# Changing the order of two TensorE products at the ends of triples in a fused attention and SwiGLU kernel

## The chip, the cores and the metric

The kernel runs on one core of one Trainium2 chip. The metric is the device time of one execution in microseconds (us), the median over several runs. A profile comes from one further execution, recorded by the hardware profiler; its span runs from the first to the last instruction. TensorE does the matrix products into PSUM banks, ScalarE (ACT in the profile) and VectorE (DVE) move and combine results, GpSimd (POOL) does small fills, and SyncE (SP) issues most DMAs.

## The reference

Two blocks follow each other. The first is a gated linear attention: per batch and head a 48 x 48 state decays by a sigmoid gate, takes in an outer product of k and v, and is read by q. The second is a SwiGLU feed-forward block on the attention's output, 3072 tokens of 384 features, with 1536 hidden features. All is float32.

```
def _attn_ref(q, k, v, f_logit):          # (4, 8, 768, 48) each
    f = 1.0 / (1.0 + np.exp(-f_logit))
    for t in range(S):
        state = f[:, :, t, :, None] * state + einsum('bhd,bhe->bhde', k[:, :, t], v[:, :, t])
        y[:, :, t] = einsum('bhd,bhde->bhe', q[:, :, t], state)

def _moe_ref(x, w_gate, w_val, w_out):    # x: (3072, 384), from y
    g = x @ w_gate
    silu = g * (1.0 / (1.0 + np.exp(-g)))
    return (silu * (x @ w_val)) @ w_out
```

## The kernel before

The sequence of 768 steps is cut into six chunks of 128 steps. A chunk of all four batches has 512 tokens. Attention works on one unit (one batch and one chunk) at a time, as a Python generator (`attention`, line 528) that hands out its work in small steps. The feed-forward block of a chunk follows one chunk or so behind, so that its matrix products fill TensorE while ScalarE and VectorE work on the attention of later chunks. Chunk 0 goes through `mlp_plain` in the usual way; chunks 1 to 5 go through `mlp_fifteen` (line 908), and it is there that the change is made.

`mlp_fifteen` computes the gate and value products with a fast scheme for a 3 x 3 by 3 x 2 block product: instead of 18 block products it makes 15, from sums of weight blocks and sums of token blocks made beforehand, and then combines the 15 results by additions into six blocks. One set of 15 is called a triple here (function `triple`, line 941); each chunk has `NJ` = 4 triples, numbered j and taken in the order 0, 2, 1, 3. The 15 products are r = 0 to 14, listed in `PRODUCTS` (line 897): each names a bank (A, B, o or c), a weight sum and a token sum. One product is four matmul records in the trace (two halves, each float32 matmul in two passes), all from line 954.

A product either opens a bank (the first use of its name in the triple, and every "o") or adds onto what is already in it. So bank A of a triple collects r0, r3, r6, r9, r12 and r14 in turn, and in between ScalarE copies its running sum out: to `c11` after r0, to `c12` after r3, and to a scratch tile `aside` after r6, r9 and r12 (line 959). Bank B is used in the same way by r1, r4, r7, r10 and r13. The next product on a bank has to wait until the copy of the one before has read it. The end of a triple and the start of the next are:

```
r12  A  a32 x t11   then ScalarE: copy A to aside
r13  B  e1 x t3     then ScalarE: copy B to aside
r14  A  a22 x b21   the bank itself is the result, read in the next triple
r0   A  a11 x t14   of the next triple, in the other A bank; then ScalarE: copy A to c11
r1   B  a23 x t8    of the next triple; then ScalarE: copy B to c22
```

There are two A banks, one B bank, two banks for o and c together, and three further banks for the attention. A bank of A is free again when the silu (line 970) and the product with it (line 906) of its triple's last result have read it; these are put off into the next triple (`late`, popped after the products in `FINISH`). Additions on VectorE that follow a product are put off by one piece (`lag`, line 905).

The order of work is written out by hand. `pieces` (line 1024) is the list of the products of a chunk's four triples; the seven products of the down projection (`down_seven`, lines 1053 and 1116) follow. Each piece has a nominal duration (`PRODUCT` = 0.86). A loop at the end of `short_path` (lines 1271 to 1280) walks through the pieces with a clock `now` that adds these up, and before each piece it lets in the attention steps whose due time has come (`come_in`). The due times are in `SCORES`, `CHAINS` and `times` (lines 825 to 841). Seven of the ends of triples inside a chunk are such due times (`between`): there the output products y (lines 649 and 653), the state products dS (694), the score products sc (615) and in the earlier chunks the transposes kt (619) come in, together with a sigmoid on ScalarE (555) that has to load its function table first, the copies of y (657), and on VectorE the mask on the scores (628) and a transpose of the sigmoid's output (561). `in_order` then fixes, for each of TensorE, VectorE, ScalarE, GpSimd and SyncE, exactly the order in which the instructions were written.

```
    now = 0.0
    for c in range(1, NCH):
        come_in(now)
        for took, f in blocks[c]:
            come_in(now)
            before = lagging[:]
            lagging.clear()
            f()
            for g in before:
                g()
            now += took
```

Of the kernel before, what the change touches and what calls it, by code (L numbers as in the profile page):

```python
# [289 lines left out]
def short_path(ctx, tc, ident, least, judge, q, k, v, f_logit, moe_w_gate, moe_w_val, moe_w_out, out):  # L290
# [595 lines left out]
    def down_weight_sums():  # L886
# [4 lines left out]
        for i in (1, 2, 4):  # L891
# [5 lines left out]
    PRODUCTS = [("A", "a11", "t14"), ("B", "a23", "t8"), ("o", "a21", "b22"),  # L897
                ("A", "a12", "t2"), ("B", "e3", "b32"), ("o", "e0", "t1"),
                ("A", "e5", "t9"), ("B", "e2", "t5"), ("c", "a13", "b11"),
                ("A", "e4", "t4"), ("B", "a33", "t15"), ("c", "a31", "t10"),  # L900
                ("A", "a32", "t11"), ("B", "e1", "t3"), ("A", "a22", "b21")]
# [3 lines left out]
    def lag(f, *args):  # L905
        lagging.append(lambda: f(*args))  # L906

    def mlp_fifteen(c):
# [28 lines left out]
        def out_part(i, n, j):  # L937
            f = i * NJ + j
            return hidden_tile(h, f % NP)[:, 2 * (f // NP) + n, :]

        def triple(j):
            p, got = {}, {}

            def both(name):
                return {"A": banks_a, "B": banks_b, "o": banks_o, "c": banks_o}[name].tile(
                    [128, 512], FP32, tag=name if name in "AB" else "o", name=name).rearrange("p (n t) -> p n t", n=2)

            def product(r):
                name, a, b = PRODUCTS[r]
                fresh = name == "o" or name not in p  # L950
                if fresh:
                    p[name] = both(name)
                for n in range(2):
                    nc.tensor.matmul(p[name][:, n, :], lhsT=weights_of[a][:, n, j, :], rhs=tokens[b],  # L954
                                     start=fresh and n == 0, stop=True, skip_group_check=True)

            def copy(name, tag, **kw):
                t = comb.tile([128, 2, TH], FP32, tag=tag, name=tag, **kw)
                nc.scalar.copy(t, p[name])  # L959
                return t  # L960

            def aside(name):
                return copy(name, "aside", bufs=3)

            def finish(i, n, src):


                def f():
                    dst = out_part(i, n, j)
                    nc.scalar.activation(dst, src[:, 0, :], AF.Silu)  # L970
                    lag(nc.vector.tensor_tensor, dst, dst, src[:, 1, :], ALU.mult)
                late.append(f)

            def one_product(r):
                product(r)
                if r in FINISH and late:
                    late.pop(0)()
                if r == 0:
                    got[11] = copy("A", "c11", bufs=2)
                elif r == 1:  # L980
                    got[22] = copy("B", "c22")
                elif r == 2:
                    lag(minus, got[22], p["o"], got[22])
                elif r == 3:
                    got[12] = copy("A", "c12")
                elif r == 4:
                    lag(plus, got[12], got[12], aside("B"))
                elif r == 5:
                    lag(minus, got[12], p["o"], got[12])
                elif r == 6:  # L990
                    lag(minus, got[22], got[22], aside("A"))
                elif r == 7:
                    got[32] = copy("B", "c32")
                elif r == 8:
                    got[31] = copy("c", "c31")
                    finish(0, 1, got[12])
                    finish(1, 1, got[22])
                elif r == 9:
                    lag(plus, got[32], got[32], aside("A"))
                elif r == 10:  # L1000
                    lag(minus, got[31], got[31], aside("B"))
                elif r == 11:
                    lag(minus, got[32], got[32], p["c"])
                    finish(2, 1, got[32])
                elif r == 12:
                    lag(minus, got[31], got[31], aside("A"))
                    finish(2, 0, got[31])
                elif r == 13:
                    lag(plus, got[11], got[11], aside("B"))
                    finish(0, 0, got[11])  # L1010
                else:
                    finish(1, 0, p["A"])

            return [(PRODUCT, lambda n=n: one_product(n)) for n in range(len(PRODUCTS))]
# [7 lines left out]
        hidden_sums, last = down_seven(c, h)  # L1022
        order = list(range(0, NJ, 2)) + list(range(1, NJ, 2))
        pieces = [f for j in order for f in triple(j)]
        half = len(PRODUCTS) * (NJ // 2)
        pieces.insert(half + 12, (0, lambda: lag(hidden_sums, 0)))
        pieces += [(0, finish_late), last[0], (0, lambda: lag(hidden_sums, 1))]
# [234 lines left out]
    def tokens_of(c):  # L1262
        token_sums, blocks[c] = mlp_fifteen(c)
        token_sums()
# [95 lines left out]
```

## Time and profile before

| | |
|---|---|
| median of 6 runs | 613.82 us (613.76 to 615.03) |
| the profiled execution | 615.0 us |
| its span | 613.3 us |
| TensorE's granted clock, mean | 0.996 |
| products of line 954 | 300, in 20 triples of 15, from 148.1 to 580.2 us |
| ScalarE's copies of line 959 | 0.58 us each |
| moved by DMA | 54.10 MB |

The page gives for each engine the time in which it ran an instruction, as a share of the span. PEld is the loading of weights, which can run while an earlier matmul is still going. The chain of waits is followed back from the last instruction: it names, at each moment, the engine that held up the end. Lines of the order of time have the start, the duration, the engine, the line, the operation, what is written and read, its shape, how many instructions are merged, and in brackets how long the engine was idle before it and what ended this.

The triples take these parts of the span, by the starts of their products: chunk 1 from 148.1 to 208.3, chunk 2 from 247.3 to 308.9, chunk 3 from 343.2 to 402.8, chunk 4 from 437.0 to 495.7 and chunk 5 from 527.8 to 580.2 us. In chunk 5 no attention is left.

### The profile page before, as it was taken

The numbers are of one execution on the slowest core, as the hardware profiler recorded it, in microseconds if no ns is written. First come the engines' busy times: TensorE is split into PE (matmuls) and PEld (weight loads), VectorE is DVE, ScalarE is ACT, GpSimd is POOL, SyncE is SP. The second block draws the span as 40 slices with busy tenths as digits, with TensorE's granted clock in tenths as the row PEclk, the third lists the DMA queues.
The fourth block names the chain that finished last, engine by engine and source line by source line (L and its number), as shares of the span: only waits on it lengthen the run. The fifth ranks groups of instructions, "written<-read, shape, count | busy, mean of one in ns | idle before, by whom it ended". The sixth has DMA issues, their size and how long they took to land.

```text
span 613.3 us, 10812 instructions
## 1 busy us (share of the span) xinstructions
PE 597.2 (97%) x4036; PEld 489.5 (80%) x4036; DVE 499.5 (81%) x882; ACT 285.3 (47%) x526; POOL 7.6 (1%) x51
## 2 busy tenths in 40 slices
PE   7799999999999999999999999999999999999996
PEld 5654545666888799888899988899988889988896
DVE  7799989878999996989997889996879992566731
ACT  2375646312776520576731376641276730366600
POOL 1000000000000000000000000000000000000000
PEclk9899999999999999999999999999999999999999
DMA  9999582005322134324235344144313100100001
GB/s 148 247 210 285 174 249 79 1 14 154 85 55 69 27 92 120 114 53 96 52 96 129 100 102 115 30 115 117 109 44 93 27 5 10 52 2 2 0 1 58
DMA packets 109142, 54.10 MB, mean 88 GB/s; under 512 B 68760, under 2 KB 102168, under 8 KB 109080
## 3 DMA queue, kind: packets, MB, share of 16 engines
q1 hardware_dynamic: 107064, 50.56, 34.7%
q10 hardware_dynamic: 2016, 2.75, 1.3%
q8 instruction: 34, 0.56, 0.4%
q14 instruction: 28, 0.23, 0.1%
HBM read 44.04 MB, written 6.29 MB: 82 GB/s over the span
## 4 chain that ended last, share of the span: by engine, by line
PE 84%; DVE 7%; DMA 3%; ACT 2%; issue 1%; SPq 1%; ACTq 0%; DVEq 0%
PE o L1053 19%; PE A L954 14%; PE B L954 11%; PE gate L752 5%; PE val L752 5%; PE o L775 5%; PE o L954 5%; PE c L954 4%; PE sc L615 4%; PE o L1116 3%; PE y L653 2%; PE y L674 2%; PE dS L694 1%; PE y L649 1%; DVE c L858 1%
## 5 line engine op out<-in xcount | busy, mean ns | idle before, releaser
L954 PE MATMUL A<-xs,w_both 128*128 128x256 f32 x240 | 62.5, 383 | 1.1 <-ACT aside L959 1.1
L1053 PE MATMUL o<-w_out,h 128*128 128x192 f32 x360 | 62.0, 328 | 0.5 <-DVE h L906 0.5
L1053 PEld LDWEIGHTS o<-w_out,h 128*128 128x128 f32 x360 | 58.7, 190 | 1.7 <-DVE h L906 0.8
L959 ACT COPY c<-A 128x512 f32<-128x512 f32 x40 | 23.3, 583 | 66.2 <-PE A L954 66.2
L954 PEld LDWEIGHTS A<-xs,w_both 128*128 128x128 f32 x240 | 44.6, 190 | 9.0 <-ACT aside L959 2.8
L855 DVE TENSOR_TENSOR c<-c,aside 128x512 f32<-128x512 f32 x60 | 41.6, 693 | 9.8 <-ACT aside L959 8.4
L959 ACT COPY aside<-A 128x512 f32<-128x512 f32 x60 | 35.0, 583 | 28.9 <-PE A L954 28.9
L906 DVE TENSOR_TENSOR h<-h,c 128x256 f32<-128x256 f32 x100 | 41.2, 420 | 7.9 <-ACT h L970 7.7
L970 ACT ACTIVATE h<-c 128x256 f32<-128x256 f32 x100 | 39.2, 416 | 9.0 <-DVE c L855 5.8
L858 DVE TENSOR_TENSOR c<-c,aside 128x512 f32<-128x512 f32 x60 | 41.3, 689 | 2.0 <-ACT aside L959 1.7
L954 PE MATMUL B<-xs,w_both 128*128 128x256 f32 x160 | 41.2, 380 | 0.7 <-ACT aside L959 0.7
L1053 PE MATMUL o<-ws,h 128*128 128x192 f32 x240 | 41.5, 328 | 0.2 <-DVE A L628 0.2
L954 PE MATMUL c<-xT,w_both 128*128 128x256 f32 x160 | 41.2, 380 | 0.5 <-DVE c L858 0.5
L954 PE MATMUL A<-xs,extra 128*128 128x256 f32 x160 | 41.2, 380 | 0.0
L954 PE MATMUL B<-xT,extra 128*128 128x256 f32 x160 | 41.1, 380 | 0.0
L959 ACT COPY aside<-B 128x512 f32<-128x512 f32 x60 | 35.0, 584 | 11.0 <-PE B L954 7.0
L628 DVE TENSOR_TENSOR A<-sc,causal 128x512 f32<-128x512 f32 x48 | 30.8, 682 | 11.2 <-PE sc L615 11.0
L1053 PEld LDWEIGHTS o<-ws,h 128*128 128x128 f32 x240 | 39.1, 190 | 0.8 <-DVE A L628 0.4
L858 DVE TENSOR_TENSOR c<-o,c 128x512 f32<-128x512 f32 x40 | 27.7, 693 | 10.2 <-ACT h L970 5.8
L954 PEld LDWEIGHTS B<-xs,w_both 128*128 128x128 f32 x160 | 30.3, 190 | 5.1 <-ACT aside L959 1.1
L954 PEld LDWEIGHTS c<-xT,w_both 128*128 128x128 f32 x160 | 30.3, 190 | 5.1 <-DVE c L858 0.9
L954 PEld LDWEIGHTS A<-xs,extra 128*128 128x128 f32 x160 | 30.3, 190 | 4.4 <-ACT c L959 0.3
(137 smaller groups left out, 1140.7 us busy)
## 6 DMA issues: line engine op xcount, KB each, us to landing
fsquares<-in_f_logit_dram SPq DMA_DIRECT2D x64, 96.0 KB, 2.7
ksquares<-in_k_dram SPq DMA_DIRECT2D x64, 96.0 KB, 2.5
qsquares<-in_q_dram SPq DMA_DIRECT2D x64, 96.0 KB, 2.2
v<-in_v_dram SPq DMA_DIRECT2D x24, 192.0 KB, 3.5
w<-in_moe_w_gate_dram SPq DMA_DIRECT2D x6, 768.0 KB, 6.1
w<-in_moe_w_val_dram SPq DMA_DIRECT2D x6, 768.0 KB, 5.4
w<-in_moe_w_out_dram SPq DMA_DIRECT2D x6, 768.0 KB, 5.6
out_dram<-ob ACTq DMA_DIRECT2D x14, 192.0 KB, 2.1
```

Source lines behind the costliest of these rows:

```text
L615: nc.tensor.matmul(sc[par][:, a * C:(a + 1) * C], lhsT=kT[r, a, :], rhs=qT[r, a, :], start=True, stop=True)
L628: nc.vector.tensor_tensor(A[:, par], sc[par].rearrange("p (a t) -> p a t", t=C), causal.unsqueeze(1).broadcast_to((128, HP, C)), ALU.mult)
L752: nc.tensor.matmul(p, lhsT=w[:, j, i, :], rhs=xT[c][:, i, :], start=(i == 0), stop=(i == KT - 1))
L775: nc.tensor.matmul(p, lhsT=hidden_tile(h, n // 2)[:, n % 2 * 2 + b // 2, b % 2 * C:(b % 2 + 1) * C], rhs=w_out[:, j, :], start=(n == 0), s ...
L855: nc.vector.tensor_tensor(dst, a, b, ALU.add)
L858: nc.vector.tensor_tensor(dst, a, b, ALU.subtract)
L906: lagging.append(lambda: f(*args))
L954: nc.tensor.matmul(p[name][:, n, :], lhsT=weights_of[a][:, n, j, :], rhs=tokens[b], start=fresh and n == 0, stop=True, skip_group_check=True)
L959: nc.scalar.copy(t, p[name])
L970: nc.scalar.activation(dst, src[:, 0, :], AF.Silu)
L1053: nc.tensor.matmul(p[:, n, :], lhsT=lhsTs[j][:, n * C:(n + 1) * C], rhs=rhs[:, j, :], start=first and j == order[0] and n == 0, stop=j == ...
L1116: nc.tensor.matmul(p, lhsT=hidden_tile(h, j)[:, 2, n * C:(n + 1) * C], rhs=b22[:, j, :], start=j == order[0], stop=j == order[-1])
```

## The change

At each end of a triple but the last of a chunk, the triple's last product r14 and the next triple's first product r0 change places in `pieces`. The new order is r12, r13, r0 of the next triple, r14, r1 of the next triple. Both have the same nominal duration, so the attention steps that came in between r14 and r0 now come in between r0 and r14. What a product brings with it moves too: the copy of r0's bank to `c11` is issued on ScalarE with r0, so ahead of the attention steps' ScalarE work; r14 issues nothing on another engine but appends a finish to `late`. There are 15 such ends. From line 1025 on, lines of the changed kernel have numbers higher by 3.

```
         pieces = [f for j in order for f in triple(j)]
+
+        for n in range(len(PRODUCTS), len(pieces), len(PRODUCTS)):
+            pieces[n - 1:n + 1] = pieces[n - 1:n + 1][::-1]
         half = len(PRODUCTS) * (NJ // 2)
         pieces.insert(half + 12, (0, lambda: lag(hidden_sums, 0)))
```

## The prediction

> **What bounds the kernel now.** I read the page's busy shares first, then the chain of waits, then what the weight loads wait for, then the order of time around the ends of triples.
>
> ```profile
> PE 597.2 (97%) x4036; PEld 489.5 (80%) x4036; DVE 499.5 (81%) x882; ACT 285.3 (47%) x526; POOL 7.6 (1%) x51
> ...
> PE 84%; DVE 7%; DMA 3%; ACT 2%; issue 1%; SPq 1%; ACTq 0%; DVEq 0%
> ```
>
> TensorE is busy for 97% of the span and carries 84% of the chain that ended last; VectorE is next. So a stall of TensorE in the triples counts in full, except where VectorE holds the pace. I number products r0 to r14 and triples 0 to 19, four for each of five token chunks. Triples 3, 7, 11, 15 and 19 are the last of their chunk and keep their order; 15 boundaries are swapped. The list of what the weight loads wait for has this row:
>
> ```profile
> PEld A L954 <- ACT aside L959: 7.7, 23, 0.7
> ```
>
> Its place is seen at the end of triple 17, where no attention work runs (order of time, all engines):
>
> ```profile
> 552.15 1.03 PE L954 MATMUL B<-xT,extra 128*128 128x256 f32 x4
> 552.40 0.58 ACT L959 COPY aside<-A 128x512 f32<-128x512 f32 x1 [1.20 <-PE A L954]
> ...
> 553.04 0.73 PEld L954 LDWEIGHTS A<-xT,w_both 128*128 128x128 f32 x4 [0.27 <-ACT aside L959]
> 553.04 1.13 PE L954 MATMUL A<-xT,w_both 128*128 128x256 f32 x4
> 553.21 0.58 ACT L959 COPY aside<-B 128x512 f32<-128x512 f32 x1 [0.22 <-PE B L954]
> ...
> 554.01 1.03 PE L954 MATMUL A<-xs,w_both 128*128 128x256 f32 x4
> ```
>
> r12 writes bank A and ScalarE copies it until 552.98; r14 adds to the same bank, with only r13 between. Its weights load at 553.04, when the copy is done, instead of about 0.21 ahead of its matmul as usual (551.93 before 552.15). From r13's start to the start after r14 are 1.86 us; two undisturbed products take 2 x 0.864 = 1.73 (the chain shows 0.86 for each r1 to r11). So this end costs 0.13 to 0.14: 0.03 of waiting and 0.10 because the next product starts with nothing loaded ahead. Where other work stands between r13 and r14 the cost is missing: the last product of triple 0 takes 0.87 (162.43 to 163.30) and of triple 16 0.88 (540.04 to 540.92). That ties it to the copy.
>
> **What the swap removes.** After r13 comes the next triple's r0, on the other A bank; then r14, with two products of cover. The copy ends 0.83 after r13 starts; r14 would now want to load at about 0.86 + 0.86 - 0.21 = 1.51 after it. Its wait goes.
>
> - Five boundaries without attention between (after triples 5, 9, 13, 17, 18): 0.14 each, 0.70.
> - Seven with attention between r14 and r0 (after triples 1, 4, 6, 8, 10, 12, 14): r13's start to the first y product is 1.96 (477.89 to 479.85). The r0 of triple 4 shows what an unstalled product before such a switch takes: 0.96 (247.25 to 248.21). So 0.864 + 0.96 = 1.82, gain 0.13 each, 0.91. The product after the attention pays the same entry after the scores (0.97) whether it is r0 or r14.
> - After triples 0 and 16: nothing to remove.
> - After triple 2: lost. There r1 of triple 3 starts at 195.21 whatever comes before, since its bank B is copied out only at 194.57 to 195.15, and that copy waited 2.14 for VectorE, which runs without a pause from 179.97. VectorE's start there waits for scores, so triple 1's gain passes through.
>
> Sum: 1.61 us.
>
> **What it adds on TensorE.** r0's new wait is for its A bank, freed by VectorE's product h<-h,A of the triple before. That ends 1.6 us (triple 1, 174.06 against 175.68) to 4.0 us (553.04 less 549.01) before r14's present start, where r0 will stand: cost 0, and a loss only if that cover shrank by 1.6. r1 still has r14 or r0 and r13's copy behind it, as now. No instruction is added; DMA issues keep their order, though SP's xT transfers wait on copies that come later (below), and xT is used only by a later chunk.
>
> **What it moves on ScalarE.** The c11 copy of r0 now enters ScalarE's queue before the sigmoid and the yT copies at the seven attention boundaries. Behind it wait a table load, the sigmoid, yT, and on VectorE the transpose that reads the sigmoid. Triple 14 is the tightest:
>
> ```profile
> 478.79 1.13 PE L954 MATMUL A<-xT,w_both 128*128 128x256 f32 x4
> 478.96 0.58 ACT L959 COPY aside<-B 128x512 f32<-128x512 f32 x1 [0.22 <-PE B L954]
> ...
> 479.56 1.28 ACT L555 ACT_TABLE_LOAD   x1
> ...
> 480.86 0.63 ACT L555 ACTIVATE fsquares<-fsquares 128x512 f32<-128x512 f32 x1
> 481.39 0.63 ACT L657 COPY yT<-y 128x256 f32<-128x256 f32 x2
> ...
> 481.58 1.11 DVE L561 STREAM_TRANSPOSE gates<-fsquares 128x512 f32<-128x512 f32 x1 [0.16 <-issue]
> ...
> 482.66 1.29 DVE L628 TENSOR_TENSOR A<-sc,causal 128x512 f32<-128x512 f32 x2
> ...
> 484.18 0.41 PEld L954 LDWEIGHTS o<-xT,w_both 128*128 128x128 f32 x2
> ```
>
> r0 will start at 477.89 + 0.86 = 478.75; its copy follows 1.07 later (as r13's: 477.89 to 478.96), at 479.82, and takes 0.60. The table load moves from 479.56 to 480.42, the sigmoid to 481.72, the transpose to 482.44, the first of the two masks to 483.52, ending (0.69 each, 0.60 apart) at 484.21. Its o bank is what r2 loads for, at 484.18 - 0.13 = 484.05. So r2 comes some 0.2 late in its load, which by the pattern of r14 costs about 0.12. I take 0.12, with 0 and 0.3 (the lateness plus a refill of 0.10) as ends. After triples 6 and 10 the same transpose stands before the mask, but TensorE does the dS products too (0.55, 264.19 to 264.74): the mask becomes free at about 390.77 against a load at 391.1: cost 0, end 0.2 each. After triples 1 and 4 the kt transposes reuse the y bank: yT's first half moves to about 265.41, kt wants it at 265.70: 0, end 0.1 each. After triples 8 and 12 the mask stands before the transpose. VectorE is then up to 0.5 late against TensorE in triples 7 and 11; the tightest reader is ScalarE's silu at 305.18, which delays the copy at 305.56 by some 0.3, and r13, which needs it, starts only at 307.08. In triple 15 VectorE has 0.68 idle before 485.88 to catch up.
>
> Net: 1.61 - 0.12 = 1.49, about 1.5 us. The profiled execution took 615.0 with a span of 613.3; by its own account it would become 613.5 with a span of 611.8. It is 1.2 slower than the median of 613.82, and taken off that median, 613.82 - 1.49 = 612.3.
>
> A rule of the Trainium skill speaks against the change. The page "ScalarE: Activation LUTs", section "What ACT_TABLE_LOAD costs", gives a switch of tables 1.28 us plus a drain of about 1.38, 2.66 in all. The row here has the load at 479.56 for 1.28 and the sigmoid at 480.86, with no drain between. With the page's sum in ScalarE's queue the mask would come 1.38 later after triples 6, 10 and 14, losing about 1.2, 1.2 and 1.7 with the refill, and kt some 1.2 twice: 6.5 lost against 1.6 gained, an estimate of 618.7. I go by the row.
>
> **The rivals.**
>
> 1. *The attention boundaries gain nothing (613.1).* If the later sigmoid and copies hold TensorE about as long as r14 did, only the plain 0.70 remains: 613.82 - 0.70. For it: the margins of 0.1 to 0.3 above, and VectorE at 81%. Against: only triple 14's margin is negative by these rows.
>
> 2. *Nothing changes (613.8).* If the 0.13 belonged to two successive products on A banks, or to r14's operands, the swap would keep it. Against: triples 0 and 16, where r14 goes at 0.87 to 0.88; for it: nothing but that those two have other work before them.
>
> 3. *Slower (615.1).* One mechanism: in-order ScalarE, at the ends of triples 6, 10 and 14. With c11 ahead of the sigmoid, transpose, mask and o bank are late and r2 waits. If the mask comes d later than worked out above, triples 7 and 11 lose d - 0.3 each, triple 15 loses d + 0.2, and each a refill of 0.10: 3d - 0.1 in all. That is more than the 1.61 gained from d = 0.57 on; at d = 1.0 it is 2.9, and the time 613.82 - 1.61 + 2.9 = 615.1. For it: the c11 copy could itself be late if r0 were held for its bank, and VectorE waits in order. Against: the bank is free 1.7 us ahead or more there, and every duration in the sum is from rows.
>
> **How the numbers follow.** Forecast 0.64, rival 1 0.20, rival 2 0.06, rival 3 0.10. The forecast's own range, from the ends (losses of 0 up to 0.3 + 0.4 + 0.2, or none and triple 2's 0.14 kept as well), is 612.1 to 613.1. The range of 611.6 to 613.6 takes in rival 1, and on the fast side half a us for what the lowest and the fifth of the six times of before differ by (613.76 and 614.25); it leaves out rival 3 and rival 2. About 0.2%, 1.2 us, is what a measurement tells from no change, so faster means below 612.6: the forecast gives 0.58 and rival 1 0.04, together 0.62; the same gets 0.29, slower 0.09.
>
> **What would show it.** In the profile after: aside-to-A waits of the weight loads fall from 23 to about 10 (13 swapped ends gone; the chunks' last triples keep theirs); r14's step is 0.86 or, after scores, 0.97; at 553 the two A products take 1.73 together; c11 copies stand before the sigmoids; a new wait of an o product for the mask in triple 15, about 0.2 long. Rows of r0 waiting for h<-h,A, of kt waiting for yT, or of o products waiting for masks in triples 7 and 11 would make the prediction wrong, as would steps of 0.97 that stay without a wait.

## The result, and the profile after

The changed kernel is faster by 0.22%: the ratio of its time to that of before is 0.9978, 95% interval 0.9973 to 0.9984 (36 and 74 runs, medians 613.63 and 614.79 us). In microseconds that is 1.0 to 1.7 less, 1.35 in the middle. The median of all 74 runs of the kernel before is higher than that of the first six, from which the prediction started (614.79 against 613.82), so the ratio is what counts: on the base of 613.82 it makes 612.5, where 612.3 was forecast. The plain ends alone, 0.70 us, would have made 0.9989, which lies outside the interval.

The page of the changed kernel, its busy times and its chain of waits:

```profile
span 611.1 us, 10812 instructions
...
PE 593.3 (97%) x4036; PEld 488.7 (80%) x4036; DVE 498.5 (82%) x882; ACT 285.6 (47%) x526; POOL 7.6 (1%) x51
...
PE 81%; DVE 10%; ACT 3%; DMA 2%; issue 2%; SPq 1%; ACTq 0%; DVEq 0%
```

TensorE still bounds the kernel; the count of instructions is the same. The list of what the weight loads wait for, of the kernel after:

```profile
PEld A L954 <- ACT aside L959: 4.1, 9, 0.7
```

Fourteen of the 23 waits of products on bank A for ScalarE's `aside` copies are gone, and 3.6 of 7.7 us. The end of triple 17 in the order of time, to be held against the same place before:

```profile
550.15 1.03 PE L954 MATMUL B<-xT,extra 128*128 128x256 f32 x4
550.40 0.58 ACT L959 COPY aside<-A 128x512 f32<-128x512 f32 x1 [1.20 <-PE A L954]
550.80 0.84 PEld L954 LDWEIGHTS A<-xs,w_both 128*128 128x128 f32 x4
551.01 1.03 PE L954 MATMUL A<-xs,w_both 128*128 128x256 f32 x4
...
551.66 0.84 PEld L954 LDWEIGHTS A<-xT,w_both 128*128 128x128 f32 x4
...
551.88 1.03 PE L954 MATMUL A<-xT,w_both 128*128 128x256 f32 x4
```

The copy of r12 ends at 550.98. r0 (A<-xs) runs meanwhile on the other A bank; r14 (A<-xT) loads at 551.66, 0.22 ahead of its matmul and with no wait in brackets. r13, r0 and r14 follow each other at 0.86 or 0.87.

How the stretch of the triples shrank, by the starts of products in the two traces (us; r13 of one triple to r1 of the next):

```
end of triple      1     2     4    5    6    8    9    10   12   13   14   16    17   18
shorter by         0.08  0.01  0.14 0.14 0.13 0.14 0.13 0.14 0.14 0.14 0.13 0.02  0.13 0.13
triple 0 to r13 of triple 19:   before 430.20    after 428.55    shorter by 1.65
```

The spans differ by 2.2, not 1.65: 0.62 of it lies ahead of the first triple, which began at 147.47 to 148.42 in the thirteen profiles of all these kernels, though no change is made before it; the stretch after r13 of triple 19, whose order is the same, was 0.13 longer, and 0.65 longer again in a second profile of the same changed kernel (35.07 and 35.72). So one span against another shows less than the ends one by one.

### The profile page after: what moved, and what is told of

Same layout as the page of the kernel before. It is cut to its first block, busy times and chain, and to the rows that moved or that the text cites. A ratio compares the mean times of both kernels' runs of the same rounds, so it can differ in the third digit from the quotient of the medians.

```text
span 611.1 us, 10812 instructions
## 1 busy us (share of the span) xinstructions
PE 593.3 (97%) x4036; PEld 488.7 (80%) x4036; DVE 498.5 (82%) x882; ACT 285.6 (47%) x526; POOL 7.6 (1%) x51
## 4 chain that ended last, share of the span: by engine, by line
PE 81%; DVE 10%; ACT 3%; DMA 2%; issue 2%; SPq 1%; ACTq 0%; DVEq 0%
PE o L1056 19%; PE A L954 14%; PE B L954 11%; PE o L954 5%; PE o L775 5%; PE val L752 4%; PE c L954 4%; PE sc L615 4%; PE gate L752 3%; PE o L1119 3%; PE y L653 2%; PE y L674 2%; PE y L649 1%; PE dS L694 1%; DVE c L858 1%
## 5 line engine op out<-in xcount | busy, mean ns | idle before, releaser
L959 ACT COPY c<-B 128x512 f32<-128x512 f32 x40 | 23.5, 586 | 26.3 <-PE B L954 22.9
```

## The experiments

They are read by the stretch from the first product of triple 0 to r13 of triple 19, and by the steps (start to start) of the products in it. Times are given as ratios to the kernel before on the same chip, with 95% intervals.

**The swap at a part of the ends.** First only where no attention comes in, then only where it does; `met` lists the latter by chunk, and the second kernel has `in met` in place of `not in met`.

```
+        met = {1: (2,), 2: (1, 3), 3: (1, 3), 4: (1, 3)}.get(c, ())
         for n in range(len(PRODUCTS), len(pieces), len(PRODUCTS)):
-            pieces[n - 1:n + 1] = pieces[n - 1:n + 1][::-1]
+            if n // len(PRODUCTS) not in met:
+                pieces[n - 1:n + 1] = pieces[n - 1:n + 1][::-1]
```

> The swap only at the eight ends of triples without attention between. I measure the stretch from the first product of triple 0 to r13 of triple 19: 430.21 us before, 428.55 with all ends swapped. Theory (r14's wait for ScalarE's copy of r12 goes, 0.14 where it was, nothing after triples 0, 2 and 16): -0.70, so 429.5, with each of the ends after triples 5, 9, 13, 17 and 18 shorter by 0.13 to 0.14. Rival (the gain comes from the c11 copy going ahead of the attention's work on ScalarE): 430.2. Time about 0.1% under before.

> The swap only at the seven ends with attention between. Theory: -0.95, so 429.25 for the same stretch, the ends after triples 4, 6, 8, 10, 12 and 14 shorter by 0.13 to 0.14 each and that after triple 1 by 0.08. Rival (the gain comes from ScalarE's order): all of the 1.66, 428.55. Time about 0.15% under before.

The first kernel took 429.36 (0.84 less), and its ratio is 0.9994 (0.9983 to 1.0005), which by itself is not clear of no change. The ends after triples 5, 9, 13, 17 and 18 ran r13, r0 and r14 at 0.86 each; the attention ends kept 0.89 to 0.92 from r13 to r14, and 1.03 to 1.06 from r14 to the first y product. The second took 429.05 (1.15 less), ratio 0.9983 (0.9972 to 0.9993), with the two groups exchanged. At the ends themselves the first gained 0.67 at those five and the second 0.81 at its seven, 0.06 instead of 0.14 at the one after triple 8; of the rest, 0.18 and 0.29 fell at the end of chunk 1, which varies from run to run (see below). So the two parts sit each in its own kind of end, and the ratios, 0.06% and 0.17%, together make about the whole. ScalarE's order is the same in the first kernel as before, instruction by instruction, so it can't have made the first group's gain.

**The suspected wait doubled, in both orders.** r12's bank is copied to `aside` a second time in all triples but the last of a chunk; the data are the same.

```
                 elif r == 12:
-                    lag(minus, got[31], got[31], aside("A"))
+                    t = aside("A")
+                    if j != 3:
+                        nc.scalar.copy(t, p["A"])
+                    lag(minus, got[31], got[31], t)
```

> Order of before; r12's copy is made twice in all triples but the last of a chunk. Theory (r14 waits for that copy): 0.58 more at each of the twelve ends that have the wait, 0.6 after triple 16, little after triples 0 and 2: 7.6 us, the stretch 437.8, the time 1.2% longer. Rival (0.13 is the price of two products on A banks in a row, or of r14's operands, and the copy does not hold it): within 0.3 of 430.2.

> Swapped order, r12's copy made twice in the same triples. Theory: with two products of cover the doubled copy ends 0.83 + 0.59 = 1.42 us after r13's start, before r14 loads at 1.52, so 428.6, at most 0.3 more through the attention ends, where r13's copy and c11 come 0.1 to 0.35 later. Rival (the swap only moves the wait): some 0.5 for each end, 434 or more.

In the old order the stretch grew by 8.0 to 438.23, ratio 1.0133 (1.0112 to 1.0153). The end of triple 17 in this kernel's order of time (L1008 is the second copy):

```profile
559.79 0.59 ACT L1008 COPY aside<-A 128x512 f32<-128x512 f32 x1
...
560.43 0.73 PEld L954 LDWEIGHTS A<-xT,w_both 128*128 128x128 f32 x4 [0.89 <-ACT aside L1008]
560.43 1.13 PE L954 MATMUL A<-xT,w_both 128*128 128x256 f32 x4 [0.48 <-ACT aside L1008]
...
561.40 1.03 PE L954 MATMUL A<-xs,w_both 128*128 128x256 f32 x4
```

r14 waits 0.89 instead of 0.27, and the step from r13 is 1.51 instead of 0.89. The difference of 0.62 is what one more copy takes, start to start (the first begins at 559.17, the second at 559.79). It came at all fourteen ends where r14 had waited; after triple 2 the next triple's r1 gave it back (the step into it fell from 1.76 to 1.15), so thirteen are left, which make 8.06. In the new order the same doubled copy, at the end of the same triple:

```profile
552.27 0.58 ACT L1008 COPY aside<-A 128x512 f32<-128x512 f32 x1
...
552.91 0.84 PEld L954 LDWEIGHTS A<-xT,w_both 128*128 128x128 f32 x4
553.12 1.03 PE L954 MATMUL A<-xT,w_both 128*128 128x256 f32 x4
```

The second copy ends at 552.85 and r14 loads at 552.91 without a wait: the two products of cover are just enough for two copies. All swapped ends kept the steps of the swapped kernel. The stretch was 429.53, 1.0 above the swapped kernel's 428.55 and so over my 0.3; against that kernel, product by product, 0.24 came in triple 1 (r11 behind the c copy), 0.24 at the end of chunk 1 (the diagonal wait, below) and 0.46 at a group of scores in chunk 2's down products (they wait for VectorE's qT), none at an end of a triple. Ratio 0.9986 (0.9974 to 0.9997).

**The c11 copy put back behind the attention's ScalarE work,** with TensorE's order as swapped.

```
+        held = []
...
+                while r == len(PRODUCTS) - 1 and held:
+                    held.pop(0)()
-                if r == 0:
+                if r == 0 and j:
+                    held.append(lambda: got.update({11: copy("A", "c11", bufs=2)}))
+                elif r == 0:
                     got[11] = copy("A", "c11", bufs=2)
```

> TensorE's order as swapped, but the c11 copy is issued on ScalarE with r14, so behind the attention's ScalarE work as before. Theory (TensorE's cover is the whole gain): the stretch of the triples stays at 428.55 within 0.1. Rival (ScalarE's order brings it): back to 430.2.

The stretch was 429.46, which is neither 428.55 nor 430.2. Product by product r13, r0 and r14 run at every end as in the swapped kernel; 0.71 of the 0.91 came at one place in chunk 1's down products and 0.21 at the scores after triple 8. The place, first in the swapped kernel and then in this one (weight loads in the order of time):

```profile
237.89 0.14 PEld L674 LDWEIGHTS y<-qT,diagonal 128*32 128x32 f32 x2 [0.24 <-ACT diagonal L545]
```

```profile
238.98 0.14 PEld L674 LDWEIGHTS y<-qT,diagonal 128*32 128x32 f32 x2 [0.95 <-ACT diagonal L545]
```

The `diagonal` tile shares its buffer with a yT tile, so its fill waits for the xT transfers that read yT; SyncE took 7.33 us to issue ten of them here and 6.46 there. The plain repeat of the swapped kernel had 0.56 at this place, so the same kernel varies here too. Its time is 0.9988 (0.9979 to 0.9997). By the ends the gain is TensorE's cover and not ScalarE's order; by the whole time alone this run would not have told.

**The c11 copy twice at the attention ends,** the mechanism of the slower rival.

```
                 if r == 0:
                     got[11] = copy("A", "c11", bufs=2)
+                    if j in {1: (1,), 2: (2, 3), 3: (2, 3), 4: (2, 3)}.get(c, ()):
+                        nc.scalar.copy(got[11], p["A"])
```

> Swapped order, the c11 copy made twice at the seven attention ends: sigmoid, yT, transpose and mask come 0.59 later. Theory of the slower rival in the prediction, with the margins that the changed kernel's trace shows: triple 15's r2 loads when the mask is done, so it loses about 0.6; in triples 7 and 11 the mask is 0.40 ahead, 0.2 to 0.3 lost each; kt after triples 1 and 4 has 0.26, about 0.3 and less lost; 1.6 in all, the stretch 430.1, the gain gone. If that queue does not reach TensorE: 428.55.

The stretch was 430.19 and the ratio 1.0010 (0.9999 to 1.0022): the gain is gone. The losses are where they were expected: 0.40 at kt after triple 1 and again after triple 4, 0.13 and 0.13 at r2 in triples 7 and 11, 0.59 at r2 in triple 15, 1.65 in all. The scores after triple 8 and those in chunk 2's down products lost 0.3 more, and the end of chunk 1 was 0.4 shorter. In triple 15 (order of time):

```profile
483.31 1.28 DVE L628 TENSOR_TENSOR A<-sc,causal 128x512 f32<-128x512 f32 x2
...
484.05 0.73 PEld L954 LDWEIGHTS o<-xT,w_both 128*128 128x128 f32 x4 [0.73 <-DVE A L628]
```

r2's load waits 0.73 for the mask. Of the delay of 0.59, 0.49 came into the step before r2, and the other 0.10 is the step after it, which begins with nothing loaded ahead. So the path over ScalarE's queue, the sigmoid and VectorE's transpose reaches TensorE, and the swapped kernel stands only some 0.1 us from it in triple 15.

**The last triples too.** A chunk's last triple has no next one to borrow from. Here r3, r6, r9 and r12 go one place earlier, so that r14 has two products of cover.

```
+        for n in range(len(pieces) - 13, len(pieces) - 1, 3):
+            pieces[n:n + 2] = pieces[n:n + 2][::-1]
...
-                if r in FINISH and late:
+                if r in (FINISH if j != NJ - 1 else (3, 5, 6, 7, 10, 11)) and late:
```

> Swapped order, and in each chunk's last triple r3, r6, r9 and r12 go one place earlier (before r2, r5, r8 and r11), so that r14 has two products of cover there too. From the first product of triple 0 to the end of the span: 463.62 in the changed kernel. Theory: 0.13 less at the ends of triples 7, 11, 15 and 19, nothing at 3 where VectorE holds the pace: 463.1. Rival (the down products then wait for VectorE's hidden values instead): 463.6 or more.

Slower than the swapped kernel: 1.0009 (0.9998 to 1.0020) against 0.9978. r14's wait is gone at all five, but a new one stands in triples 7, 11 and 15 (order of time, triple 7):

```profile
298.43 1.28 ACT L970 ACT_TABLE_LOAD   x1
...
300.05 0.57 ACT L959 COPY c<-A 128x512 f32<-128x512 f32 x1
...
300.67 0.73 PEld L954 LDWEIGHTS A<-xs,extra 128*128 128x128 f32 x4 [0.69 <-ACT c L959]
```

r3's finish loads the silu table and runs a silu ahead of r3's copy, and r6, now a place closer, waits for that copy: 1.31 and 0.97 where 0.86 were, 0.56 lost for 0.14 gained. It was not the wait for VectorE that I had as rival. In triple 3 r13 came 0.41 late behind an `aside` copy, and the end of chunk 1 was 0.6 longer. In triple 19, with no sigmoid before it, all steps are 0.86.

**The table loaded early.** The same pattern stands in the kernel before, in triples 0, 4, 8 and 12 (r11 1.31, r12 0.97). One silu on a single column, issued after r5, pulls the load into an idle gap.

```
+    flat = const.tile([128, 1], FP32, tag="flat", name="flat")
...
+                if r == 5 and j == 0:
+                    nc.scalar.activation(flat, ones[:, 0:1], AF.Silu)
```

> Swapped order, and one silu on a 128 x 1 tile after r5 of each chunk's first triple, so that ScalarE loads the table in an idle gap of 1.14 us instead of between r8's and r9's copies. In triples 0, 4, 8 and 12 r12 waits for r9's copy: r11 takes 1.31 and r12 0.97 instead of 0.86. Theory: 0.56 less in each of the four, the stretch from triple 0 to the end 461.4, the time 0.35% under the changed kernel. Rival (those triples then wait for VectorE or the turn transfers): less than 0.5 gained.

The stretch was 427.14, 1.4 under the swapped kernel, and the ratio 0.9953 (0.9940 to 0.9966, five runs), the best of all. ScalarE in triple 8, first in the swapped kernel and then in this one (order of time; lines of the old code are higher by 2 here, and L981 is the new silu):

```profile
350.59 1.28 ACT L970 ACT_TABLE_LOAD   x1
...
352.21 0.57 ACT L959 COPY aside<-A 128x512 f32<-128x512 f32 x1
```

```profile
346.30 1.28 ACT L981 ACT_TABLE_LOAD   x1
347.60 0.20 ACT L981 ACTIVATE flat<-ones 128x1 f32<-128x1 f32 x1
...
350.01 0.59 ACT L961 COPY aside<-A 128x512 f32<-128x512 f32 x1
```

The last line of each is the copy of r9, for which r12 waits. The wait of r12 is gone in all four triples (steps 0.86). Of the 0.56 each, triple 12 kept 0.55, triples 0 and 4 about 0.3, and triple 8 0.02: there the scores after it took 0.5 longer, behind VectorE, which frees their o bank. That loss isn't tied to the early load: in the last run below, whose kernel has the same order of work up to chunk 5, triple 8 kept its 0.55 too. From triple 0 to the end of the span it was 462.81, not the expected 461.4; the last run below had 461.38.

**Both, with r3's silu behind its copy.** To the edits of the last two, one line moves in a chunk's last triple: the pop of `late` at r3 goes behind the copy to c12. Beside it the swap alone was run once more.

```
                 elif r == 3:
                     got[12] = copy("A", "c12")
+                    if j == NJ - 1:
+                        late.pop(0)()
```

> The swap, the table loaded early in the first triples, and the last triples reordered as in the run with the last triples, but with r3's silu issued behind r3's copy, since there r6 waited 0.45 for that copy behind the silu's table load (the step before it 1.31, the next 0.97) in triples 7, 11 and 15. From triple 0 to the end of the span: 462.81 with the table alone. Theory: 0.13 less at the ends of triples 7, 11, 15 and 19 and up to 0.2 in triple 3: 462.1 to 462.3, apart from the wait of the y products for the diagonal tile at the end of chunk 1, which differs by up to 0.7 between runs. Rival (the silu behind the copy makes VectorE and the down products late): 462.8 or more.

> The changed kernel once more, beside the run with table and last triples on one chip, as the measure for it. The ends of triples as in the first profile: 12 steps of r14 at 0.86, or 0.96 before the y products, and 0.9978 of the time of before. Theory for the pair: the other is 0.2% to 0.3% faster than this one.

The two together were slower: 1.0021 (1.0012 to 1.0029), while the swap alone beside it had 0.9977 (0.9963 to 0.9991) again, with the same steps at all its ends as in the first profile. r6's wait is gone, but in triples 7, 11 and 15 r13 now loads late. In triple 7 (order of time):

```profile
306.32 0.42 ACT L972 ACTIVATE h<-c 128x256 f32<-128x256 f32 x1 [1.49 <-DVE c L860]
306.65 0.57 ACT L961 COPY aside<-B 128x512 f32<-128x512 f32 x1
...
307.26 0.73 PEld L956 LDWEIGHTS B<-xT,extra 128*128 128x128 f32 x4 [1.27 <-ACT aside L961]
```

A silu waits 1.49 for VectorE, the copy of r10 stands behind it in ScalarE's queue, and r13 behind the copy: the rival, by way of ScalarE. r13 came 1.03 late in triples 7 and 11 and 0.44 in triple 15.

**The table early, and the last triple of chunk 5 alone.** To the edit with the table loaded early comes the reordered last triple, in chunk 5 only, with r3's finish ahead of r3's copy as in the first run of the last triples.

```
-                if r in FINISH and late:
+                if r in (FINISH if j != NJ - 1 or c != NCH - 1 else (3, 5, 6, 7, 10, 11)) and late:
...
+        for n in range(len(pieces) - 13, len(pieces) - 1, 3) if c == NCH - 1 else ():
+            pieces[n:n + 2] = pieces[n:n + 2][::-1]
```

> The swap, the table loaded early in the first triples, and the reordered last triple in chunk 5 alone, where no attention is left and the reordered triple ran all its steps at 0.86. From triple 0 to the end 462.81 with the table alone; theory 0.13 less, 462.7 within the 0.7 by which the diagonal wait at the end of chunk 1 differs between runs, and a ratio of 0.994 to 0.997 to before, under the 0.9977 of the swap alone. Rival (the early table load gains nothing in time, its one measurement was luck): 0.9975 to 0.998.

The ratio was 0.9965 (0.9953 to 0.9977, six runs), the stretch 426.57. So two kernels with the early table lie at 0.9953 and 0.9965, below both measurements of the swap, though the interval of the second touches that of the swap (0.9973). In the profiles the stretch is 1.4 to 2.3 shorter than in the swap's two (428.55 and 428.90).

## Why the prediction was right, point by point

*What bounds the kernel, and the wait removed.* Right, and shown by the doubled copy: r14 waits for r12's copy, one more copy costs 0.62 in the old order and nothing at the ends in the new one. The count of waits fell from 23 to 9 where about 10 was forecast: the one after triple 16 (0.16) was in the list as well. The second rival (the price belongs to two products on A banks or to r14's operands) falls with it, since r0 and r14, both on A banks, still follow each other, at 0.86.

*The size at the plain ends.* 0.14 each forecast, 0.13 to 0.14 measured at all five; nothing after triple 0, 0.02 after 16.

*The size at the attention ends.* 0.13 each forecast, 0.13 to 0.14 measured at six. The term for triple 1 was too large: 0.08. There r13 itself loads 0.20 late, behind r10's copy, so r14's wait was shorter than elsewhere, 0.21 instead of 0.27; I had read the size from triple 14 and counted seven alike.

*Triple 2's gain lost.* Right: r1 of triple 3 begins 0.01 earlier relative to triple 2's r13. VectorE holds that place, and the step into r1 grew from 1.76 to 1.89.

*r0's new wait for its A bank.* Cost 0, as forecast; it never appears among the waits.

*ScalarE's moved copy.* The chain was right, the one price in it was not: I took 0.12 for r2 in triple 15 and it was 0. In the order of time of the kernel after:

```profile
476.92 1.03 PE L954 MATMUL A<-xs,w_both 128*128 128x256 f32 x4
...
477.98 0.59 ACT L959 COPY c<-A 128x512 f32<-128x512 f32 x1 [0.28 <-PE A L954]
...
478.58 1.28 ACT L555 ACT_TABLE_LOAD   x1
...
479.88 0.63 ACT L555 ACTIVATE fsquares<-fsquares 128x512 f32<-128x512 f32 x1
...
480.60 1.11 DVE L561 STREAM_TRANSPOSE gates<-fsquares 128x512 f32<-128x512 f32 x1 [1.03 <-issue]
...
481.56 1.27 DVE L628 TENSOR_TENSOR A<-sc,causal 128x512 f32<-128x512 f32 x2
...
482.28 0.76 PEld L954 LDWEIGHTS o<-xT,w_both 128*128 128x128 f32 x4
482.42 1.03 PE L954 MATMUL o<-xT,w_both 128*128 128x256 f32 x4
```

From r0 to the transpose every step came as worked out (1.06, 0.60, 1.30, 0.72). The mask followed the transpose after 0.96, where I had taken 1.08 from the trace of before; there the mask had been waiting for the scores, so that gap was no duration. The load at 482.28 is still 0.07 later than 0.21 ahead of its matmul, and the loads ran closer together (four in 0.76 instead of 0.84), so that nothing was lost; the wait of about 0.2 there, which was named as a sign, came as these 0.07. The first rival, no gain at the attention ends, falls with this and with the run of the attention ends alone; it wasn't far off, as the doubled c11 copy shows. That run also bears out the third rival's mechanism: with d = 0.59 the formula 3d - 0.1 for the three r2 gave 1.7, and 0.85 was lost there, since each of the three masks had 0.26 to 0.30 more room than I had given it (0.39, 0.39 and 0.89 expected, 0.13, 0.13 and 0.59 lost); kt, left out of the formula, lost 0.80. Its sign would have turned at about the delay that was tried.

*The sum.* Forecast 1.61 - 0.12 = 1.49; the trace shows 1.65 and the times 1.35 (1.0 to 1.7). By terms: the plain ends gave 0.67 (forecast 0.70), the attention ends 0.89 (0.91, triple 1 short by 0.05 and the other six together 0.03 over), the end after triple 16 0.02, and some 0.07 came in triple 3 and behind it in chunk 1, where the waits were a little shorter; the 0.12 wasn't paid. That the whole came within 0.2 of the forecast is in part luck, since the 0.12 and the 0.05 are misses in opposite directions. As to the rule of the Trainium skill that spoke against the change ("ScalarE: Activation LUTs", section "What ACT_TABLE_LOAD costs", which adds a drain of about 1.38 us to each load of 1.28): the trace after shows the load 0.01 behind the copy and the sigmoid 1.30 after the load's start at the new place too, so no drain, and the measurement decides.

## What to carry to other kernels

When a product adds onto a bank that another engine still copies out, count the products between: here the copy is done 0.83 us after the next product starts and a product lasts 0.86, so with the weights loaded 0.21 ahead one product of cover costs 0.14 and two cost nothing. An exchange with the next group's first product bought the cover here at no cost, since that product has another bank, which was free in time; but look at what its copy is now ahead of in its engine's queue, and add up that chain to the next bank that TensorE needs. A stall of this kind that can't be exchanged away (the last triples) may only move, as it did there: each copy that comes a place closer has to be looked at with whatever stands before it in its queue, a table load above all.

## What the runs showed that I had not expected

- A weight load that came 0.07 late cost nothing in triple 15: its matmul still began on time, and the four loads took 0.76 instead of 0.84.
- A 1.28 us table load between two of ScalarE's copies cost TensorE 0.56 in each of four triples of the kernel before, four times the wait that the change was about; one silu on a single column in an idle gap took those waits away, though only about 1.2 of 2.2 us stayed gained in the one profile and 1.7 in the other.
- The end of chunk 1 varies between runs by up to 0.7 us (the wait for `diagonal` 0.24 in the swapped kernel, 0.56 in its repeat and 0.95 with the c11 copy put back). In the first and the last of these SyncE took 6.46 and 7.33 us to issue ten small transfers. Why it varies stays open. It is a half of what the change is worth, and one reason why kernels that differ by 0.1% aren't told apart by one profile's span.
- Ten profiles have the end of triple 8 in the new order. Six of them lost 0.04 to 0.53 at the scores there, and in these six VectorE's additions at that place took 0.72 to 0.77 us each; in the four without a loss they took 0.67 to 0.69. The kernels differ in other things too, so a cause is not shown by this, and why the additions take longer in some runs stays open.
